# Start of an attention and MLP kernel: the zeros of the first products are cleared first, and the first q is loaded over three queues, ahead of the identity

## The chip, the cores and the metric

One core of one Trainium2 chip runs the whole program. The metric is device time in microseconds, the median of several runs. Engines are called as in the profile: PE (TensorE, with PEld for its weight loads), DVE (VectorE), ACT (ScalarE), POOL (GpSimd) and SP (SyncE, which here only issues DMAs). POOL, SP and ACT each issue DMAs in the order of their own program.

## The reference

```
scores = q @ k.T / sqrt(64)              # 4 x 12 heads, 448 x 448, head size 64
scores = cap * tanh(scores / cap)        # cap = 30
attn   = exp(scores - max) / (sum + 1e-9)
x      = (attn @ v), heads side by side  # 1792 x 768
h      = relu(x @ w_in)                  # w_in  768 x 2048, float64
out    = (h * h) @ w_out                 # w_out 2048 x 768, float64
```

## The kernel before, in words

The twelve heads of each of four batches are taken in pairs: 24 steps `n`, each with two heads. A head has 448 keys and 448 queries, which lie on the partitions as seven blocks of 64. Products that must be exact are made of float32 values split in a high and a low part (`hi`, `lo`, tiles `kqh` and `kql`), in three products.

In one step of the main loop PE transposes the next pair's k and q (`transpose_k`, `transpose_q`, lines 334 to 345), against the identity matrix `ident`, into PSUM. `take` (lines 347 to 354) splits the result; `scores` (L362) multiplies k by q; ACT applies tanh (L369) and exp (L374); `pv` and `pv_half` (L397, L389) multiply by v. Weights of the MLP are decoded from float64 beside that, and the MLP's first products (`hps`, L286) begin while attention still runs. The second products of the MLP (`po`, L654 to L656) end the program.

Ahead of the main loop stands a prologue, and the change lies wholly in it:

- `make_identity` (its lines carry the name masks.py in the profile) fills `ident` on POOL: a memset of zeros (masks.py:197), then an affine select that writes the ones of the diagonal (masks.py:199).
- DVE clears padding of the k and v buffers and writes ones beside v (L231 to L237), and then `zero` (L433).
- PE multiplies `zero` by `zero` NWARM = 9 times into a PSUM tile `warm` that nobody reads (L436); the profile shows each of these products as two matmuls.
- `load_k(0)`, `load_q(0)` (L305, L306, L315, L316) load the first pair, half on SP's queue, half on ACT's. `cap`, the q of step 1, and the v of steps 0 and 1 are loaded on POOL's queue (L440, L315, L316, L305, L306), the k of step 1 and the first weights on SP's.
- The first transposes, the split of their results (`take` with ACT's copy and DVE's subtraction), and some one-column arithmetic on `cap` follow.

The prologue is not written in its order on the engines: a scheduler places each instruction on its engine's list when the program is built, and the engine then runs that list in order. The main loop stands under a manual schedule, in the order in which it is written.

Of the kernel before, what the change touches and what calls it, by code (L numbers as in the profile page):

```python
# [10 lines left out]
F32 = mybir.dt.float32  # L11
# [158 lines left out]
def tile_softcap_attention_mlp(ctx, tc, q, k, v, cap, w_in, w_out, out):  # L170
    nc = tc.nc
# [3 lines left out]
    P = 128  # L175
# [10 lines left out]
    NWARM = 9  # L186
    NKQ = 2
# [18 lines left out]
    g_dram = dram.tile([NF, P, NT], F32, name="g_dram", bufs=1)  # L206

    ident = const.tile([P, P], F32, name="ident")
    make_identity(nc, ident)
    cap_sb = const.tile([P, 1], F32, name="cap_sb")  # L210
    ncap = const.tile([P, 1], F32, name="ncap")
    qks = const.tile([P, 1], F32, name="qks")
# [3 lines left out]
    keep = actx.enter_context(tc.tile_pool(name="keep", bufs=1))  # L216
# [2 lines left out]
    ps_s = actx.enter_context(tc.tile_pool(name="ps_s", bufs=2, space=PSUM))  # L219
    ps_t = actx.enter_context(tc.tile_pool(name="ps_t", bufs=1, space=PSUM))  # L220
    ps_v = actx.enter_context(tc.tile_pool(name="ps_v", bufs=2, space=PSUM))

# [2 lines left out]
    kn, qn, vn = [], [], []  # L227
# [71 lines left out]
    top, bottom = slice(0, D), slice(D, P)  # L299
# [8 lines left out]
    def load_k(n, queues=(nc.sync, nc.sync)):  # L308
        load_keys(kn[n % NKQ], k, n, queues)

    def load_q(n, queues=(nc.sync, nc.sync)):
        b, j = divmod(n, NPAIR)
        for i in range(2):
            x = q[b, 2 * j + i].rearrange("(p t) d -> p t d", t=NS)
            queues[i].dma_start(out=qn[n % NKQ][top, 0:4, i], in_=x[:, 0:4])  # L315
            queues[i].dma_start(out=qn[n % NKQ][bottom, 0:3, i], in_=x[:, 4:7])  # L316

    def load_v(n):
        load_keys(vn[n % NKV][:, :, :, 0], v, n, (nc.gpsimd, nc.gpsimd))
# [108 lines left out]
        last["dve"] = nc.vector.tensor_sub(out=lo, in0=x, in1=hi.bitcast(F32))  # L428
        xh[b, j], xl[b, j] = hi, lo


    zero = keep.tile([P, P], F32, name="zero")
    nc.vector.memset(zero, 0.0)  # L433
    warm = ps_t.tile([P, 512], F32, tag="t", name="warm")
    for _ in range(NWARM):
        nc.tensor.matmul(out=warm[:, :P], lhsT=zero, rhs=zero, start=True, stop=True)  # L436
    both, pool = (nc.sync, nc.scalar), (nc.gpsimd, nc.gpsimd)
    load_k(0, both)
    load_q(0, both)
    nc.gpsimd.dma_start(out=cap_sb, in_=cap.partition_broadcast(P))  # L440
    load_k(1)
    load_q(1, pool)
    load_v(0)
    load_v(1)
# [37 lines left out]
    with tc.manual_schedule(engines={E.PE, E.Activation, E.DVE, E.Pool}):  # L482
# [13 lines left out]
        for n in range(NP + 1):  # L496
# [54 lines left out]
            if n + 2 < NP:  # L551
                load_k(n + 2)
                load_q(n + 2)
                load_v(n + 2)
# [165 lines left out]
```

## Time and profile before

| | |
|---|---|
| runs, us | 719.66, 720.54, 721.70 (median 720.54) |
| profiled execution, us | 720.83 |
| its span, first to last instruction, us | 719.1 |
| mean granted clock of TensorE | 0.994 |
| busy: PE, DVE, ACT, POOL | 98%, 58%, 44%, 12% |

The profiled execution took 720.83 us, of which 719.1 us lie between its first and its last instruction; the other 1.7 us lie around them. Busy shares are of the span. All stretches below are in microseconds from the start of the span. A "granted clock" of 1.00 stands for 2.4 GHz and 0.50 for 1.2 GHz.

### The profile page before, as it was taken

What the parts mean: (1) busy time and instruction counts of PE and PEld (TensorE: products, weight loads), DVE (VectorE), ACT (ScalarE), POOL (GpSimd) and SP (SyncE); (2) the same over time, 40 slices, a digit from 0 to 9 for tenths busy, and PEclk for the clock granted to TensorE, in tenths of its full rate; (3) what the DMA queues carried; (4) which work ended last, traced back from release to release, by engine and by line L of the source; (5) the groups of instructions that cost most, each with busy time, mean ns of one, the idle gap of its engine ahead of it and who ended that gap; (6) DMA issues with size and microseconds to landing.
All of it is one profiled execution on the core that took longest, in us unless ns stands there. A gap on an engine that the chain in (4) does not pass through costs nothing.

```text
span 719.1 us, 10204 instructions
## 1 busy us (share of the span) xinstructions
PE 701.3 (98%) x3642; PEld 589.7 (82%) x3642; DVE 414.3 (58%) x882; ACT 315.8 (44%) x454; POOL 88.6 (12%) x131
## 2 busy tenths in 40 slices
PE   6999999999999999999999999999999999999995
PEld 4655666666566679989999999999999999999995
DVE  4687878778776664548899989419971111111100
ACT  5787777678766743135344444224432111111100
POOL 6432334234232002010000000000000000000000
PEclk9999999999999999999999999999999999999998
DMA  8335544354343033137456454436645232222111
GB/s 168 94 92 123 120 111 114 90 129 111 96 117 100 16 82 136 65 131 223 152 171 192 156 194 157 150 110 183 186 122 152 81 87 80 81 81 82 27 29 27
DMA packets 110334, 83.01 MB, mean 115 GB/s; under 512 B 56449, under 2 KB 100993, under 8 KB 110273
## 3 DMA queue, kind: packets, MB, share of 16 engines
q1 hardware_dynamic: 103840, 73.53, 36.2%
q0 software_dynamic: 3232, 5.74, 3.4%
q10 hardware_dynamic: 3200, 2.98, 1.3%
q8 instruction: 31, 0.51, 0.3%
q14 instruction: 31, 0.25, 0.1%
HBM read 61.87 MB, written 20.27 MB: 114 GB/s over the span
## 4 chain that ended last, share of the span: by engine, by line
PE 91%; DVE 4%; ACT 1%; DMA 1%; issue 1%; SPq 0%; ACTq 0%
PE hps L286 33%; PE pv L397 14%; PE po L654 11%; PE po L655 11%; PE po L656 11%; PE sc L362 7%; PE pv L389 2%; PE tp L338 1%; DVE kql L354 1%; DVE kqh L353 1%; PE sc L344 1%; ACT p L369 1%; DMA kn<-in_k_dram 1%; PE warm L436 1%; PE sc L345 0%
## 5 line engine op out<-in xcount | busy, mean ns | idle before, releaser
L286 PE MATMUL hps<-xs,kqh 128*128 128x448 f32 x576 | 163.7, 365 | 1.3 <-DVE r L291 1.3
L654 PE MATMUL po<-ohi,gh 128*128 128x384 f32 x448 | 149.7, 335 | 0.6 <-ACT osb L661 0.6
L655 PE MATMUL po<-olo,gh 128*128 128x384 f32 x448 | 150.0, 335 | 0.0
L656 PE MATMUL po<-ohi,gl 128*128 128x384 f32 x448 | 148.4, 335 | 0.0
L397 PE MATMUL pv<-p,vn 128*128 128x448 f32 x288 | 122.1, 560 | 0.0
L286 PEld LDWEIGHTS hps<-xs,kqh 128*128 128x128 f32 x576 | 108.1, 188 | 10.2 <-DVE r L291 1.7
L369 ACT ACTIVATE p<-sc,qks 128x896 f32<-128x896 f32 (+1 forms) x96 | 86.7, 904 | 57.5 <-DVE kql L354 42.0
L286 PE MATMUL hps<-xs,kql 128*128 128x448 f32 x288 | 105.2, 365 | 0.0
L607 DVE TENSOR_TENSOR gl<-graw,gh 128x2048 fp32r<-128x2048 f32 x14 | 32.1, 2292 | 124.1 <-ACT gh L606 114.3
L397 PEld LDWEIGHTS pv<-p,vn 128*128 128x128 f32 x288 | 51.2, 191 | 51.3 <-issue 42.1
L374 ACT ACTIVATE p<-p,cap_sb 128x896 f32<-128x896 f32 (+1 forms) x96 | 91.3, 951 | 2.1
L654 PEld LDWEIGHTS po<-ohi,gh 128*128 128x128 f32 x448 | 84.0, 188 | 0.9 <-ACT osb L661 0.9
L655 PEld LDWEIGHTS po<-olo,gh 128*128 128x128 f32 x448 | 84.1, 188 | 0.0
L656 PEld LDWEIGHTS po<-ohi,gl 128*128 128x128 f32 x448 | 83.9, 188 | 0.0
L290 ACT ACTIVATE r<-hps 128x448 f32<-128x448 f32 x64 | 34.6, 541 | 76.2 <-PE hps L286 74.5
L606 ACT CAST gh<-graw 128x2048 fp32r<-128x2048 f32 x14 | 26.7, 1910 | 91.9 <-PE po L655 81.8
L291 DVE TENSOR_TENSOR r<-hps,r 128x448 f32<-128x448 f32 x64 | 39.7, 621 | 43.2 <-ACT r L290 43.1
L44 ACT ACTIVATE mag<-wraw 128x384 f32<-128x384 f32 x64 | 34.8, 552 | 53.4 <-DVE olo L56 31.0
L286 PEld LDWEIGHTS hps<-xs,kql 128*128 128x128 f32 x288 | 54.1, 188 | 4.3
L286 PE MATMUL hps<-xs,whi 128*128 128x448 f32 x192 | 56.1, 372 | 0.0
L362 PE MATMUL sc<-kqh 64*128 64x448 f32 (+1 forms) x168 | 43.6, 441 | 2.9 <-ACT p L369 2.0
L661 ACT COPY osb<-po 128x384 f32<-128x384 f32 x28 | 13.2, 477 | 69.9 <-PE po L656 59.2
(85 smaller groups left out, 843.2 us busy)
## 6 DMA issues: line engine op xcount, KB each, us to landing
g_dram<-r SPq DMA_DIRECT2D x64, 224.0 KB, 2.5
graw<-g_dram SPq DMA_DIRECT2D x14, 1024.0 KB, 5.8
wraw<-in_moe_w_in_dram SPq DMA_DIRECT2D x32, 384.0 KB, 4.0
wraw<-in_moe_w_out_dram SPq DMA_DIRECT2D x32, 384.0 KB, 3.6
rb<-rd SPq DMA_DIRECT2D x24, 224.0 KB, 3.5
vn<-in_v_dram POOLq DMA_DIRECT2D x48, 64.0 KB, 3.4
kn<-in_k_dram SPq DMA_DIRECT2D x47, 64.0 KB, 2.6
qn<-in_q_dram SPq DMA_DIRECT2D x45, 64.0 KB, 2.6
```

Of the source, the lines that this page charges most:

```text
L44: yield nc.scalar.activation(out=magf, in_=high.bitcast(F32), func=ACTF.Abs, scale=2.0 ** 16)
L286: nc.tensor.matmul(out=ps, lhsT=w[:, c * P:(c + 1) * P], rhs=x[b, c], start=(n == 0), stop=(n == 3 * KDM - 1))
L290: nc.scalar.activation(out=r, in_=ps, func=ACTF.Relu)
L291: last["square"] = nc.vector.tensor_mul(out=r, in0=ps, in1=r)
L362: nc.tensor.matmul(out=sc[:, h, :S], lhsT=kx[r, t * P:(t + 1) * P], rhs=qx[r, 4 * P:], start=(s == 0), stop=(s == 2))
L369: nc.scalar.activation(out=p, in_=probs[n, u][:, :c, :S], func=ACTF.Tanh, scale=qks)
L374: nc.scalar.activation(out=p, in_=p, func=ACTF.Exp, scale=cap_sb)
L397: nc.tensor.matmul(out=pvs[n, h], lhsT=vs[:, u - 1, h].rearrange("p a d -> p (a d)"), rhs=p[:, h], start=(u == 1), stop=(u == 3))
L607: nc.vector.tensor_sub(out=gl, in0=graw, in1=gh.bitcast(F32))
L654: nc.tensor.matmul(out=po[:, o, :HO], lhsT=gh, rhs=hi[:, os_], start=(f == 0), stop=False)
L655: nc.tensor.matmul(out=po[:, o, :HO], lhsT=gh, rhs=lo[:, os_], start=False, stop=False)
L656: nc.tensor.matmul(out=po[:, o, :HO], lhsT=gl, rhs=hi[:, os_], start=False, stop=(f == NF - 1))
```

## The change

Two pieces of the prologue move, and the queues of one load change.

```diff
     ident = const.tile([P, P], F32, name="ident")
-    make_identity(nc, ident)
...
     ps_v = actx.enter_context(tc.tile_pool(name="ps_v", bufs=2, space=PSUM))
+
+    zero = keep.tile([P, P], F32, name="zero")
+    nc.vector.memset(zero, 0.0)
+    warm = ps_t.tile([P, 512], F32, tag="t", name="warm")
+    for _ in range(NWARM):
+        nc.tensor.matmul(out=warm[:, :P], lhsT=zero, rhs=zero, start=True, stop=True)
...
-    def load_q(n, queues=(nc.sync, nc.sync)):
+    def load_q(n, upper=(nc.sync, nc.sync), lower=None):
         b, j = divmod(n, NPAIR)
         for i in range(2):
             x = q[b, 2 * j + i].rearrange("(p t) d -> p t d", t=NS)
-            queues[i].dma_start(out=qn[n % NKQ][top, 0:4, i], in_=x[:, 0:4])
-            queues[i].dma_start(out=qn[n % NKQ][bottom, 0:3, i], in_=x[:, 4:7])
+            upper[i].dma_start(out=qn[n % NKQ][top, 0:4, i], in_=x[:, 0:4])
+            (lower or upper)[i].dma_start(out=qn[n % NKQ][bottom, 0:3, i], in_=x[:, 4:7])
...
-    zero = keep.tile([P, P], F32, name="zero")
-    nc.vector.memset(zero, 0.0)
-    warm = ps_t.tile([P, 512], F32, tag="t", name="warm")
-    for _ in range(NWARM):
-        nc.tensor.matmul(out=warm[:, :P], lhsT=zero, rhs=zero, start=True, stop=True)
     both, pool = (nc.sync, nc.scalar), (nc.gpsimd, nc.gpsimd)
     load_k(0, both)
-    load_q(0, both)
+    load_q(0, (nc.gpsimd, nc.scalar), (nc.gpsimd, nc.sync))
+    make_identity(nc, ident)
     nc.gpsimd.dma_start(out=cap_sb, in_=cap.partition_broadcast(P))
```

What the scheduler makes of it is seen in the engines' lists. Line numbers of the changed kernel are higher by 5 or 6 in the load functions (L305 becomes L311, L315 becomes L321). First POOL's list before, from its first row after the branch to the program: `qn1` is the q of step 1, `vn0` the v of step 0.

```order
masks.py:197 MEMSET ident_79 128x128
L440 DMA cap_sb_84<-in_cap_dram 128x1
L315 DMA qn1_112<-in_q_dram 64x4x64
L316 DMA qn1_112<-in_q_dram 64x3x64
masks.py:199 ISA
masks.py:199 AFFINE_SELECT ident_79<-ident_79 128x128
L315 DMA qn1_112<-in_q_dram 64x4x64
L316 DMA qn1_112<-in_q_dram 64x3x64
L305 DMA vn0_115<-in_v_dram 64x4x64
```

The affine select stands behind three DMA issues. In the changed kernel POOL's list begins so (`qn0` is the q of step 0):

```order
L321 DMA qn0_116<-in_q_dram 64x4x64
L322 DMA qn0_116<-in_q_dram 64x3x64
masks.py:197 MEMSET ident_79 128x128
L441 DMA cap_sb_80<-in_cap_dram 128x1
L321 DMA qn1_120<-in_q_dram 64x4x64
L322 DMA qn1_120<-in_q_dram 64x3x64
```

Two more issues of `qn1` follow, four of `vn0` and two of `vn1`, and then these rows (`vn1` and `vn2` are the v of steps 1 and 2):

```order
L311 DMA vn1_127<-in_v_dram 64x3x64
L312 DMA vn1_127<-in_v_dram 64x4x64
masks.py:199 ISA
masks.py:199 AFFINE_SELECT ident_79<-ident_79 128x128
L311 DMA vn2_131<-in_v_dram 64x4x64
```

The affine select has moved behind fifteen DMA issues: the two of the first q, the one of `cap`, four of the next q, and eight of v. PE's list, with what each row waits for, begins in the changed kernel with the products of zeros and the transposes of k, then those of q (`Pool`, `DVE` and `PE` are the engines' semaphores, DMAHW those of loads from SP and ACT, DMASW those of loads from POOL):

```order
L227 MATMUL warm<-zero 128x128 [waits DVE_49]
L227 MATMUL warm<-zero 128x128 x8
L344 MATMUL tp<-ident,kn_115 128x128 [waits DMAHW1_49,DMAHW2_49,DMAHW0_49,DMAHW3_49,PE_49,Pool_49]
L344 MATMUL tp<-ident,kn_115 128x128 x2
L344 MATMUL tp<-ident,kn_115 128x128 [waits DVE_49]
L350 MATMUL tp<-ident,qn_116 128x128 [waits DMAHW4_49,DMAHW5_49,DMASW1_49,DMASW0_49]
```

Before, the transposes of q stood ahead of those of k; the first transposes wait for POOL, that is for `ident`, in both kernels. On DVE the clearing of `zero` moves from behind twelve memsets to the head of the list. On ACT and on SP one load of the first q goes to POOL from each pair of theirs; SP's reading of the flag `far` (L597, L598 in the changed kernel) moves from behind the loads of steps 2 and 3 to ahead of them. From the first scores on, the lists of PE, DVE, ACT and POOL are the same in both kernels.

## Rows read from the trace of the kernel before

**Rows 1.** The profile's page: busy time, share of the span and instructions of each engine; and the shares of the span in the chain of work that ended last, by engine.
```profile
PE 701.3 (98%) x3642; PEld 589.7 (82%) x3642; DVE 414.3 (58%) x882; ACT 315.8 (44%) x454; POOL 88.6 (12%) x131
...
PE 91%; DVE 4%; ACT 1%; DMA 1%; issue 1%; SPq 0%; ACTq 0%
```

**Rows 2.** The chain that ended last, in order of time, in the first 20 us: start, duration, what. Consecutive pieces follow one another without a gap.
```profile
0.83 0.11 DVE kn L231
...
4.05 0.15 DVE zero L433
4.20 0.04 issue
4.25 4.02 PE warm L436 x18
8.27 0.33 PE tp L344 x3
...
8.83 0.54 ACT kqh L353
...
9.40 0.62 DVE kql L354
...
10.04 0.70 DVE kql L354
...
10.79 0.49 PE sc L362 x2
...
11.30 1.02 ACT p L369
...
12.34 1.05 ACT p L374
13.39 0.90 ACT p L369
...
15.21 3.20 PE pv L397 x8
```

**Rows 3.** The timeline of POOL in the first 12 us: start, duration, engine, line, operation. Between 3.58 and 11.52 stand twelve more DMA issues with no gap.
```profile
0.75 0.20 POOL masks.py:197 MEMSET ident<- 128x128 f32 x1 [0.29 <-POOLq L702]
1.30 0.72 POOL L440 DMA_DIRECT2D cap_sb<-in_cap_dram  x1 [0.34 <-issue]
2.02 0.63 POOL L315 DMA_DIRECT2D qn<-in_q_dram  x1
2.63 0.62 POOL L316 DMA_DIRECT2D qn<-in_q_dram  x1
3.34 0.30 POOL masks.py:199 TENSOR_SCALAR_AFFINE_SELECT ident<-ident 128x128 f32<-128x128 f32 x1
3.58 0.64 POOL L315 DMA_DIRECT2D qn<-in_q_dram  x1
...
11.52 0.63 POOL L306 DMA_DIRECT2D vn<-in_v_dram  x1
```

**Rows 4.** The timeline of PE between 7.9 and 12 us: the transposes of the first q and k.
```profile
8.10 0.49 PE L344 MATMUL tp<-ident,qn 128*128 128x128 f32 x3
...
8.73 0.66 PE L338 MATMUL tp<-ident,kn 128*128 128x128 f32 x4
```

**Rows 5.** The timeline of the first 20 us, all engines: the third DMA issue of ACT and of SP.
```profile
2.20 0.64 ACTq L315 DMA_DIRECT2D qn<-in_q_dram  x1
...
2.47 0.64 SPq L315 DMA_DIRECT2D qn<-in_q_dram  x1
```

**Rows 6.** Busy time of each engine by stretch: the stretch, its length, then PE, PEld, DVE, ACT, POOL busy (with the number of instructions), the granted clock of TensorE, the busy share of the DMA engines, GB/s.
```profile
4.25:8.30 4.05, 4.05 (x20) 4.05 (x21) 0.87 (x8) 0.78 (x2) 4.05 (x7) 1.00 1.11 199
...
66.00:69.00 3.00, 1.57 (x13) 0.97 (x12) 1.50 (x5) 2.74 (x4) 0.00 (x0) 1.00 0.39 87
69.70:72.60 2.90, 2.90 (x9) 1.54 (x8) 2.80 (x6) 2.87 (x4) 1.00 (x1) 0.50 0.12 23
...
711.40:714.50 3.10, 0.00 (x0) 0.00 (x0) 0.00 (x0) 0.48 (x1) 0.00 (x0) 1.00 0.28 74
714.50:719.10 4.60, 0.00 (x0) 0.00 (x0) 0.00 (x0) 0.00 (x0) 0.00 (x0) 0.50 0.03 7
```

**Rows 7.** The chain that ended last, in order of time, between 60 and 76 us: products with v in the stretch of the lower granted clock.
```profile
70.72 2.75 PE pv L397 x4
```

**Rows 8.** DMA issues of the first 12 us by tile and queue: number, KB each, median us from issue to landing.
```profile
qn<-in_q_dram POOLq DMA_DIRECT2D x2, 64.0 KB, 3.9
...
qn<-in_q_dram SPq DMA_DIRECT2D x1, 48.0 KB, 4.3
cap_sb<-in_cap_dram POOLq DMA_DIRECT2D x1, 0.5 KB, 3.3
```

**Rows 9.** Who waited for whom, PE alone, from 8 us to the end: us in total, times, longest.
```profile
PE sc L362 <- ACT p L369: 2.0, 3, 0.7
PE hps L286 <- DVE r L291: 1.3, 1, 1.3
PE pv L389 <- DVE vl L324: 1.1, 2, 0.6
```

**Rows 10.** Groups of instructions by line and form in the first 15 us, ACT's copy of the first k: busy time, mean ns of one, idle time before it.
```profile
L353 ACT CAST kqh<-tp 128x512 fp32r<-128x512 f32 x1 | 0.6, 585 | 0.1
```

**Rows 11.** Who waited for whom, SP's queue, first 30 us: us in total, times, longest.
```profile
SPq L305 <- PE tp L338: 1.6, 1, 1.6
```

## The prediction

> **What bounds the kernel now.** I read the page's busy shares first, then the chain that ended last. PE is busy for 701.3 of 719.1 us, and 91% of the chain lies on it [rows 1]: a reader should see that whatever makes PE start its real work later is paid at the end in full, unless a wait further on gives it back. PE's waits behind the start are few, and each is released by ACT or DVE (2.0, 1.3 and 1.1 us) [rows 9], whose work comes from PE's own products, so they move along with it. None waits for a clock of its own, such as a long load. I take it that a delay at the start reaches the end one to one.
>
> Then the chain of the first microseconds, which is where the change lies. DVE clears `zero` last of its memsets, ready at 4.20; the products of zeros run from 4.25 to 8.27; the transposes of q follow at once [rows 2]. So before, the first transposes wait for the products of zeros, and these for DVE. `ident` is no part of that chain: its affine select starts at 3.34 and lasts 0.30, so it is there by 3.65 [rows 3], 4.4 us before the first transpose at 8.10 [rows 4].
>
> **The change, part by part.**
>
> *Zeros first.* The products of zeros can start some 3.2 us earlier: DVE's first memset begins at 0.83 [rows 2], `zero` takes 0.15 to 0.17, so PE starts near 1.05 and, at the 4.02 us of before [rows 2], ends near 5.1. Taken alone this is the gain of the change, at most 3.2 us. The other memsets move back by 0.17 us, hidden behind loads that land later.
>
> *The first q.* It loses one issue each on ACT and SP and gets two on POOL. Landing takes 3.9 us from POOL and 4.3 from SP [rows 8]. With the first issue on POOL at 0.75 and the third ones on ACT and SP at about 2.2 and 2.5 [rows 5], all of k and q is there by about 6.8 us. With the zeros done at 5.1, the transposes would start at 6.8 instead of 8.1 if loads were all they waited for.
>
> *The identity.* They aren't. POOL's list puts the affine select behind fifteen DMA issues, and in the trace POOL is held by each issue: in a row of them the next starts 0.61 us later (3.58 to 11.52 is thirteen steps, 7.94 us), and the affine select of before started only when the three issues ahead of it were over, at 3.34 after 2.63 plus 0.62 [rows 3]. So I add up: start 0.75; two issues of the first q at 0.72 (the first on this queue) and 0.62, to 2.09; the memset 0.20 and the pause of 0.34 that followed it, to 2.63; `cap` 0.62, to 3.25; twelve issues at 0.61, to 10.58; a gap of 0.09 ahead of the affine select and its 0.30, to 10.97; a few hundredths to PE. The first transpose starts at about 11.0 instead of 8.1: **+2.9 us**. Bounds: without the pause and with 0.60 per issue 10.5 (+2.4); with 0.64 per issue and some 0.3 of waits for an earlier load's semaphore 11.7 (+3.6). I take the middle, since the row of thirteen steps is the very same kind of issue on the same queue.
>
> *The order of k and q.* k's transposes now come first. From the first transpose to the last wait of the first scores, before: 8.08 to 10.79, 2.71 us [rows 2]. After: k's transposes 0.66 [rows 4], ACT's copy of k 0.585 [rows 10] and of q 0.54, then DVE's second subtraction, 0.62 for q [rows 2], with some 0.1 of steps between: about 2.6. DVE's subtraction of k, 0.70 [rows 2], runs beside ACT's copy of q. I cost it at nothing.
>
> *TensorE's clock.* PE now stands idle from about 5.1 to 11.0. The trace shows what such idleness does: the last product ends at 711.4, the granted clock stays at 1.00 to 714.5, and from there it is 0.50, the 1.2 GHz level [rows 6]. It even fell inside the loop, at 69.7, behind a stretch of 3 us in which PE was busy for 1.57 [rows 6]. So I take the low level for the first work behind the pause. What that costs: four products with v took 2.75 us in the low stretch [rows 7], eight took 3.20 in the other [rows 2], 0.69 against 0.40 each. On the path at the start stand k's transposes (0.66, doubled less a little overlap: +0.55) and the last pair of the first scores (0.49: +0.45), so +1.0. Behind that ACT needs 1.02, 1.05 and 0.90 us for tanh, exp and tanh [rows 2], 2.97 in all, and PE has some 2.7 us of products in this time; doubled they stick out by up to 2.4 us if the level doesn't rise. In the trace it was low for 2.9 us in the loop [rows 6], and at the start it rose within the 4.02 us of the zeros. The path behind the first transpose reaches the end of the first scores about 4 us later, so I let most of ACT's cover hold and take **+1.2 us**, between 0 (the level is up again at once) and 3.4 (1.0 and 2.4).
>
> The granted clock of the very start reads 1.00 [rows 6], and yet the 18 matmuls of zeros took 4.02 us [rows 2], 0.223 us for 128 columns, where eight products with v took 0.40 for 448, that is 0.114 for 128: half the speed, so the low level, which the column doesn't show there. The Trainium skill ("TensorE: Matmul & The Clock Gate", Part 1) says that the slow clock is the default and that "activity releases the throttle". By the granted clock of that row the pause would cost nothing and the sum would be 723.4; by the page's rule it costs a second ramp, 724.6; the durations of these rows bear out the rule.
>
> *The rest.* SP reads `far` earlier, a single instruction ahead of the k loads of step 2, which wait for the first transposes of k anyway (1.6 us) [rows 11]: nothing. The v loads of step 2 leave POOL about 2 us later, and are wanted two steps on: nothing. `cap` is issued at 2.63 instead of 1.30, lands 3.3 us later [rows 8], and is wanted by the first tanh, near 15: nothing.
>
> **The sum.** 720.83 (the profiled execution, of which 719.1 is the span) plus 2.9 plus 1.2 is 724.9. That execution stands 0.29 above the median of the three runs, 720.54; on the median's footing I predict **724.6 us**. About 0.3%, 2.2 us, is what a measurement of this kernel can tell from no change.
>
> **The rivals.**
>
> - *The clock doesn't matter* (0.10). The identity is late, but the level is high when PE resumes or rises at once. For it speaks the granted clock of 1.00 at the start; against it the fall 3.1 us behind the last product [rows 6]. 720.54 plus 2.9: 723.4.
> - *The low level lasts* (0.06). PE has short pauses for ACT and DVE in its first work, as it had in the 3 us ahead of 69.7 [rows 6], and the level stays low past the cover: 2.9 plus 3.4, 726.8.
> - *A part of the delay is given back* (0.06). One of PE's waits, or the fall at 69.7, which doubles products on the chain [rows 7], doesn't come at the shifted time. The four products alone gave up 1.15 us there, and with their neighbours and a wait of 1.3 it makes up to 2.5: 722.1.
> - *The identity isn't late* (0.04). POOL hands its issues on without being held, and the affine select runs soon after its memset. Then the loads bound the first transpose, at 6.8 instead of 8.1: 720.54 less 1.3 is 719.2, no slower than before. The point from which it decides: the affine select would have to end by 8.0, so fifteen issues would have to cost no more than 0.42 us each (8.0 less 0.30, 0.09, 0.54 and 0.75 is 6.3). The row shows 0.61 and an affine select that waited for the issues ahead of it [rows 3], which is why it gets so little.
>
> The Trainium skill ("DMA: Bandwidth & Descriptors", Issuing engines are not separate DMA queues) has a rule on that side: starting loads on several engines saves only the time of issuing them, which is usually small beside the load. By it the issues would hardly hold POOL, and the last rival would be the likeliest; the 0.61 us of an issue [rows 3] against 3.9 us to landing [rows 8] says that fifteen of them are not small here.
>
> **How the numbers follow.** The forecast has the remaining 0.74. Its own bounds are 2.4 to 3.6 for the identity and, for the larger part, 0.6 to 2.0 for the clock: 723.5 to 726.1. The first three rivals add 722.1 to 726.8, and the fall at 69.7 may come or not in either kernel. The range for 8 times in 10 is **722.4 to 727.0**; the identity in time, and part of the two cases at its ends, are left out. Slower by over 0.3% means above 722.7: nearly all of the forecast, most of the first rival and the second, 0.87. Within 0.3%: the identity in time, most of the part given back, and a few hundredths of the others, 0.11. Faster by over 0.3%, below 718.4: only if an identity in time meets a clock that never falls, 0.02.
>
> **What would show it right or wrong.** In the changed kernel's POOL timeline the affine select should start at about 10.7, right behind the eighth load of v, and the first transpose at about 11.0; PE's zeros should run from about 1.05 to 5.1, and then nothing for nearly 6 us. The chain should begin with POOL's issues instead of DVE's memsets. The granted clock should read 0.50 for a few us at the start, and k's first four transposes take about 1.2 instead of 0.66. From there the timeline should be that of before, shifted by about 4 us to the end. I am wrong on the identity if the affine select starts before 9, on the clock if the first transposes run at 0.66, and on carrying the delay if the last product doesn't end 3 to 5 us later than 711.4.

## The result, and the profile after

The changed kernel takes 725.40 us, the median of six runs from 724.68 to 726.30; beside it the kernel before took 721.34 (719.66 to 721.85). The medians differ by 4.1 us. The ratio on record is 1.0061, with a 95% interval of 1.0048 to 1.0074: slower. Like all ratios below it is worked out from the single runs, and can differ from the quotient of the two medians by up to 0.2%. The profiled execution took 725.12 us with a span of 723.4, against 720.83 and 719.1.

The page's first row and its chain by engine, which answer to [rows 1], show PE still busy nearly throughout, with 1.2 us more of work and a span that is 4.3 us longer:

```profile
PE 702.5 (97%) x3642; PEld 590.9 (82%) x3642; DVE 414.5 (57%) x882; ACT 315.6 (44%) x454; POOL 90.2 (12%) x133
...
PE 89%; DVE 5%; DMA 2%; ACT 1%; issue 1%; SPq 1%; ACTq 0%
```

Then the timeline of POOL in the changed kernel, which answers to [rows 3]: start, duration, line, operation, and in brackets the idle time before it and what ended it.

```profile
1.28 0.76 POOL L321 DMA_DIRECT2D qn<-in_q_dram  x1 [0.82 <-POOLq L703]
2.03 0.63 POOL L322 DMA_DIRECT2D qn<-in_q_dram  x1
2.65 0.22 POOL masks.py:197 MEMSET ident<- 128x128 f32 x1
2.79 0.59 POOL L441 DMA_DIRECT2D cap_sb<-in_cap_dram  x1
3.38 0.62 POOL L321 DMA_DIRECT2D qn<-in_q_dram  x1
...
10.09 0.62 POOL L312 DMA_DIRECT2D vn<-in_v_dram  x1
10.81 0.30 POOL masks.py:199 TENSOR_SCALAR_AFFINE_SELECT ident<-ident 128x128 f32<-128x128 f32 x1
```

Twelve issues lie from 3.38 to the end of the one at 10.09, 0.61 us each, and only then comes the affine select. It ends at 11.11. PE in the same stretch, which answers to [rows 4]:

```profile
1.07 4.21 PE L227 MATMUL warm<-zero 128*128 128x128 f32 x18 [1.07 <-DVE zero L224]
11.16 1.12 PE L344 MATMUL tp<-ident,kn 128*128 128x128 f32 x4 [5.88 <-DMA wraw<-in_moe_w_in_dram]
12.07 0.85 PE L350 MATMUL tp<-ident,qn 128*128 128x128 f32 x3
...
13.84 0.74 PE L368 MATMUL sc<-kqh 64*128 64x448 f32 x2 [0.62 <-ACT kqh L359]
...
15.04 0.58 PE L368 MATMUL sc<-kqh,kql 64*128 64x448 f32 x2
```

and the first weight loads of the transposes:

```profile
11.16 0.72 PEld L344 LDWEIGHTS tp<-ident,kn 128*128 128x128 f32 x4 [6.18 <-POOL ident masks.py:199]
```

The zeros run from 1.07 to 5.28, PE stands idle for 5.88 us, and four transposes take 1.12 us instead of 0.66. The two rows name different releasers: the row of the matmuls a load of weights that happened to land at 11.14, the row of the weight loads POOL's `ident`, ready at 11.11. The chain of the changed kernel follows the first of the two and shows 4.69 us of that load, and not POOL's issues, as I had forecast. A chain follows whatever came last, to a few hundredths of a microsecond, and can be led away by a coincidence; the experiments with the identity settle which of the two it was.

The first tanh of ACT answers to the piece at 11.30 in [rows 2]:

```profile
15.66 1.01 ACT L375 ACTIVATE p<-sc,qks 128x896 f32<-128x896 f32 x1 [1.87 <-PE sc L368]
```

It comes 4.36 us later. From there I laid ACT's first tanh of each step side by side in the two timelines:

| step | before, us | after, us | later by |
|---|---|---|---|
| 0 | 11.30 | 15.66 | 4.36 |
| 3 | 38.49 | 42.85 | 4.36 |
| 5 | 58.76 | 62.87 | 4.11 |
| 6 | 69.81 | 74.56 | 4.75 |
| 9 | 99.69 | 103.97 | 4.28 |
| 12 | 131.94 | 136.28 | 4.34 |
| 23 | 249.44 | 253.79 | 4.35 |

The last product starts at 715.38 instead of 711.03, 4.35 us later; the first line is of the changed kernel, the second of the kernel before:

```profile
715.38 0.34 PE L657 MATMUL po<-ohi,gl 128*128 128x384 f32 x1
```

```profile
711.03 0.34 PE L656 MATMUL po<-ohi,gl 128*128 128x384 f32 x1
```

So in this pair of executions the loss is complete before the first tanh and stays to the end. Only steps 5 to 9 wander, between 4.11 and 4.75 us, as is described below under the rival that a part is given back.

### The profile page after: what moved, and what is told of

The parts are those of the page before. It is cut to its first block, busy times and chain, and to the rows that moved or that the text cites. A ratio compares the mean times of both kernels' runs of the same rounds, so it can differ in the third digit from the quotient of the medians.

```text
span 723.4 us, 10209 instructions
## 1 busy us (share of the span) xinstructions
PE 702.5 (97%) x3642; PEld 590.9 (82%) x3642; DVE 414.5 (57%) x882; ACT 315.6 (44%) x454; POOL 90.2 (12%) x133
## 4 chain that ended last, share of the span: by engine, by line
PE 89%; DVE 5%; DMA 2%; ACT 1%; issue 1%; SPq 1%; ACTq 0%
PE hps L292 33%; PE pv L403 13%; PE po L655 11%; PE po L656 11%; PE po L657 11%; PE sc L368 7%; PE pv L395 2%; PE tp L344 1%; DVE kql L360 1%; DMA cmp<-e 1%; DVE kqh L359 1%; PE sc L350 1%; DVE x L430 1%; DMA wraw<-in_moe_w_in_dram 1%; ACT p L375 1%
```

## The experiments

All times are medians; "before" was run beside each group, with 721.05, 721.07 and 721.25 us in the three groups. The first table collects what the sections speak of: the start of the affine select, of the first transposes and of the first tanh in the profile, and the ratio to before with its 95% interval. A profiled execution is one of the runs and need not lie at the median: e1's is the slowest of its seven, 720.27, and so is b3's, 720.60.

| kernel | affine select | first transpose | first tanh | median | ratio to before |
|---|---|---|---|---|---|
| before | 3.34 | 8.10 | 11.30 | 721.34 | |
| changed | 10.81 | 11.16 | 15.66 | 725.40 | 1.0061 (1.0048 to 1.0074) |
| e1, identity early | 3.37 | 5.34 | 9.48 | 718.91 | 0.9968 (0.9955 to 0.9981) |
| e2, zeros only | 3.35 | 5.41 | 11.47 | 720.83 | 0.9993 (0.9982 to 1.0003) |
| e7, queues only | 3.36 | 8.24 | 11.44 | 720.29 | 0.9996 (0.9988 to 1.0005) |
| e6, behind seven | 5.94 | 6.30 | 10.79 | 719.89 | 0.9989 (0.9978 to 1.0000) |
| e5, behind eleven | 8.39 | 8.76 | 13.24 | 723.29 | 1.0030 (1.0021 to 1.0038) |
| e4, 36 zeros | 10.81 | 12.11 | 15.38 | 723.91 | 1.0039 (1.0024 to 1.0055) |
| e8, 31 zeros | 10.80 | 11.16 | 14.46 | 723.38 | 1.0028 (1.0016 to 1.0040) |
| b1, v ahead | 3.38 | 5.43 | 9.07 | 723.33 | 1.0034 (1.0017 to 1.0050) |
| b2, v ahead, 13 zeros | 3.39 | 6.43 | 9.94 | 721.68 | 1.0008 (0.9994 to 1.0021) |
| b3, q of step 1 split | 3.36 | 5.52 | 9.80 | 719.39 | 0.9968 (0.9957 to 0.9979) |
| b4, the same, 11 zeros | 3.37 | 5.43 | 9.35 | 718.92 | 0.9985 (0.9966 to 1.0004) |

**The identity early.** The changed kernel, with nothing but the identity's place on POOL's list undone:

```diff
-    make_identity(nc, ident)
+    with tc.high_priority():
+        make_identity(nc, ident)
```

> The changed kernel with the identity alone given priority: POOL's list has its memset first and its affine select behind three DMA issues instead of fifteen; zeros first and the three queues stay. My theory (POOL is held 0.61 us by each issue ahead of the affine select, and TensorE's clock falls in the long pause): the affine select starts near 3.4, the loads bound the first transpose at about 6.8, the pause behind the zeros is only 1.5 us and the transposes run at 0.66 for four. 1.3 us below the kernel before, about 720.0 by a median of 721.3. Rival one, that it is q's way over POOL's queue that is late: the first transpose stays near 11 and the time near 725.4. Rival two, that the clock falls even in a short pause: about 721.3, like before.

PE's timeline:

```profile
1.07 4.12 PE L227 MATMUL warm<-zero 128*128 128x128 f32 x18 [1.07 <-DVE zero L224]
5.34 0.63 PE L344 MATMUL tp<-ident,kn 128*128 128x128 f32 x4
6.33 0.52 PE L350 MATMUL tp<-ident,qn 128*128 128x128 f32 x3 [0.37 <-DMA qn<-in_q_dram]
...
8.33 0.73 PE L368 MATMUL sc<-kql,kqh 64*128 64x448 f32 x2 [0.18 <-DVE kql L360]
```

The time falls to 718.91, 6.5 us below the changed kernel and 2.1 below before, where I had expected 1.3. So the identity's place on POOL's list is what turned the change from a gain to a loss, and it was `ident`, not the load of weights, that released the transposes. The loads of q bound them now, at 6.33 rather than the 6.8 I expected. The first rival is refuted. Of the second a part is true: the clock was up for the first transposes (0.63 for four) and low again in the first scores (0.73, then 0.58 for a pair), but the time isn't the 721.3 that it named. Where the 2.1 us come from no trace shows: in the profiled execution, the slowest of the seven, the first tanh comes 1.82 us sooner than before, that of step 1 only 0.63, and the last product 0.33 (710.70). A part of the lead is lost to v:

```profile
PE pv L403 <- DMA vn<-in_v_dram: 0.7, 2, 0.4
```

**Single parts.** The zeros first alone (the clearing and the products of zeros move together), and then the three queues alone, each on the kernel before:

```diff
     ps_v = actx.enter_context(tc.tile_pool(name="ps_v", bufs=2, space=PSUM))
+    zero = keep.tile([P, P], F32, name="zero")
+    nc.vector.memset(zero, 0.0)
...
-    zero = keep.tile([P, P], F32, name="zero")
-    nc.vector.memset(zero, 0.0)
...
     both, pool = (nc.sync, nc.scalar), (nc.gpsimd, nc.gpsimd)
```

> The kernel before with only the clearing of zero and its products moved first; q on SP and ACT, the identity early. My theory: zeros end near 5.2, the last load of q (fourth issue on SP at 3.15, 4.3 us to landing) bounds the first transpose at about 7.5 instead of 8.1, so 0.6 us below before, about 720.7. Against the run with the identity early it prices the three queues alone, 0.7 us. Rival (zeros first is what costs, since the clock falls before the transposes): 1 us or more above before.

The chain of that run:

```profile
3.14 4.48 DMA qn<-in_q_dram
7.62 0.24 issue
7.86 0.87 PE tp L349 x3
```

As expected the fourth issue on SP bounds the transposes of q, at 7.86. But they ran at the low level, 0.87 for three, and so had those of k, which follow the zeros directly:

```profile
5.41 1.09 PE L343 MATMUL tp<-ident,kn 128*128 128x128 f32 x4
```

The first tanh came at 11.47, 0.17 later than before. The median is 0.2 us lower, not to be told from none: for the zeros alone no gain is shown.

```diff
-    load_q(0, both)
+    load_q(0, (nc.gpsimd, nc.scalar), (nc.gpsimd, nc.sync))
```

> The kernel before with only the first q over three queues; identity early, zeros last. Theory: the first transposes still wait for the zeros, at 8.1, so nothing is gained; POOL issues two loads more ahead of v, so the v of step 0 comes 1.2 us later, and since the first product with v waited 0.3 us for it before, up to 1.2 us are lost: 721.1 to 722.3. Rival (the three queues are a gain of their own): below 720.4.

The median, 720.29, lies below the 720.4 that the rival had named, but before stood at 721.07 beside it and the interval of the ratio reaches 1, so no gain is shown. Nor does the start show one: the zeros end at 8.41, against 8.27 before, and the first tanh comes 0.14 us later. Nothing was lost either: PE's list of waits in that run holds none for v. The 1.2 us that I allowed for the later v were not paid: it was issued 1.2 us later and still in time.

**How many issues ahead.** The changed kernel with v's loads put behind the affine select, those of steps 1 and 2 (eleven issues stay ahead, the diff) or also `load_v(0)` under the same `issue_after` (seven):

```diff
-    make_identity(nc, ident)
+    nc.gpsimd.memset(ident, 0.0)
+    ones = nc.gpsimd.affine_select(out=ident, in_=ident, compare_op=ALU.not_equal, fill=1.0, base=0,
+                                   pattern=[[-1, P]], channel_multiplier=1)
...
-    load_v(1)
+    with tc.issue_after(ones.ins):
+        load_v(1)
...
-                load_v(n + 2)
+                with tc.issue_after(ones.ins):
+                    load_v(n + 2)
```

> The changed kernel with the v loads of steps 1 and 2 put behind the affine select on POOL's list: it stands behind eleven issues instead of fifteen. My theory: it starts 4 x 0.61 us earlier, at 8.4, and the first transpose at 8.7. The pause behind the zeros is then about 3.4 us, near what ended with a fall at the end of the program (3.1), so the clock is open: with a fall 723.0, without 721.7. Rival, that the affine select waits for loads to land and not for issues: it starts at another time than 8.2 to 8.6. Rival, that only a handful of issues ahead matter: it stays near 10.8 and the time near 725.4.

> The changed kernel with all v loads put behind the affine select: it stands behind seven issues. By the 0.61 us an issue (10.81 behind fifteen, 8.39 behind eleven) it should start at 5.95 and end at 6.26, just when the last load of the first q is there (6.3 with the identity early). So this is the point from which the identity stops to bound: first transposes at 6.3, about 0.4 us later than with the identity early (719.3 against 718.9). If the identity were still the bound in another way (a fixed lateness behind any load), it would lie well above 720.

The affine select in the two runs, eleven issues first:

```profile
8.39 0.31 POOL L441 TENSOR_SCALAR_AFFINE_SELECT ident<-ident 128x128 f32<-128x128 f32 x1
```

```profile
5.94 0.31 POOL L441 TENSOR_SCALAR_AFFINE_SELECT ident<-ident 128x128 f32<-128x128 f32 x1
```

and the first transposes behind them, in the same order:

```profile
8.76 1.11 PE L344 MATMUL tp<-ident,kn 128*128 128x128 f32 x4 [3.47 <-POOL ident L441]
```

```profile
6.30 1.12 PE L344 MATMUL tp<-ident,kn 128*128 128x128 f32 x4 [1.02 <-POOL ident L441]
```

With 10.81 behind fifteen that is 2.42 and 2.45 us for four issues, 0.61 each: POOL is held by the issue, not by the landing. Both forecasts of the start hold to 0.02 us. Behind eleven the first transpose comes at 8.76, the level is low (1.11 for four transposes) and the median 723.29, near the 723.0 of the case with the low level. Behind seven, `ident` is ready when the last load of q is, but it still bounds the start: the transposes of k, which began at 5.34 with the identity early, wait for it until 6.30 and then run at the low level, and the first tanh comes 1.31 us later than there. The median is 719.89, against the 719.3 expected and 718.91 with the identity early. So seven issues are not yet the point from which the identity costs nothing.

**The clock.** The changed kernel with more products of zeros, so that PE has no pause, or a short one, ahead of the identity; first 36, then 31:

```diff
-    NWARM = 9
+    NWARM = 36
```

> The changed kernel with 36 products of zeros instead of 9, nothing else. My theory: 9 to 10 of them at the low level to about 5, the others at 0.21 us each, to about 10.7; the first transpose stays at 11.16, since the identity bounds it, but the clock is up: four transposes of k in 0.66 instead of 1.12, first tanh 3.2 us behind the first transpose instead of 4.5. 1.3 us below the changed kernel, about 724.1. Rival, that the 1.3 us come from the order of k and q or from loads beside them and not from the clock: 725.4, tanh still 4.5 behind. If the zeros run past 11.1 the gain is smaller by what they run over.

> The changed kernel with 31 products of zeros: with 36 they ran on to 12.0, past the identity (11.1), since the low level lasted longer than I had reckoned. At 0.213 us each five fewer end at 10.9. Then the identity bounds the first transpose again, at 11.16, and only the clock differs from the changed kernel: first tanh 3.25 us behind the first transpose, at 14.4, instead of 15.66; 1.25 us below the changed kernel, about 724.1, or 3.0 above before. Rival (the clock is not what makes the difference of 1.3): 725.4.

With 36 they ran to 12.0, past the identity, because the low level lasted longer than I had reckoned; the first transpose came 0.95 us late. From there to the first tanh it is 3.27 us, against 4.50 in the changed kernel, but the price of the clock is not read cleanly from it. With 31:

```profile
1.07 9.26 PE L227 MATMUL warm<-zero 128*128 128x128 f32 x62 [1.07 <-DVE zero L224]
11.16 0.66 PE L344 MATMUL tp<-ident,kn 128*128 128x128 f32 x4 [0.83 <-POOL ident masks.py:199]
11.65 0.49 PE L350 MATMUL tp<-ident,qn 128*128 128x128 f32 x3
...
12.96 0.47 PE L368 MATMUL sc<-kqh 64*128 64x448 f32 x2 [0.62 <-ACT kqh L359]
...
14.05 0.36 PE L368 MATMUL sc<-kqh,kql 64*128 64x448 f32 x2
```

```profile
14.46 1.01 ACT L375 ACTIVATE p<-sc,qks 128x896 f32<-128x896 f32 x1 [1.55 <-PE sc L368]
```

The first transpose starts at 11.16, as in the changed kernel to the hundredth, and the first tanh at 14.46 instead of 15.66. So 1.20 us of the loss are TensorE's clock, and the order of k and q and the loads beside it are not to blame. The medians differ by 2.0 us, 0.8 more, and whether that too is the clock is not shown. In the two profiles e8 is ahead of the changed kernel by 1.20 us at the first tanh of step 0 and by 1.22 in step 3, behind it by 0.62 in steps 4 and 5, and ahead by 1.64 from step 6 on: 0.4 us of the rest come in where both wander.

**A better version.** With the identity early PE waited 0.7 us for v, as shown above. Two ways to bring v forward: ahead of the q of step 1, or with a part of that q on ACT's queue.

```diff
     load_k(1)
-    load_q(1, pool)
     load_v(0)
+    load_q(1, pool)
     load_v(1)
```

> Identity early, zeros first, three queues, and on POOL's list the v of step 0 ahead of the q of step 1. With the identity early the first tanh came 1.82 us sooner than before, the second only 0.63: PE waited 0.7 us for v at the first products with v. With v four issues (2.4 us) sooner this wait should go: 718.2 against 718.9. Rival: the q of step 1, now 2.4 us later, is waited for instead, and nothing is gained or something lost.

> As the run with v ahead, with 13 products of zeros instead of 9, so that PE has no pause between the zeros and the last load of q (5.2 to 6.3). If the low level in the first scores (products of 0.58 instead of 0.37 us) comes from these pauses, it goes in most executions, and the first tanh comes up to 0.7 us sooner: about 717.5. If the level's return hangs on something else than these pauses: 718.2 to 718.9, as without.

The rival came true, that q is then waited for. PE's timeline in the run with nine zeros:

```profile
13.66 0.52 PE L350 MATMUL sc<-ident,qn 128*128 128x128 f32 x3 [2.66 <-DMA qn<-in_q_dram]
```

The first tanh was the earliest of all, at 9.07, and was given back to a wait of 2.66 us for the q of step 1, whose loads were issued from 6.1 to 8.5 and took 4.6 to 5.7 us to land. The first tanh of step 1 came only 0.17 us sooner than before. With 13 zeros this wait is 2.46. Both medians lie above before, that of b2 by an amount not told from none. The wait explains why the lead is gone, not why b1's median is 2.3 us above before: the profiled execution, 720.70, is the second fastest of twelve that reach from 720.17 to 725.92. The six with a mean granted clock of 0.991 or 0.992 took 722.51 to 725.92, so a longer time at the low level goes with much of the loss; no trace shows where. The other way:

```diff
-    load_q(1, pool)
+    load_q(1, (nc.gpsimd, nc.scalar))
```

> The run with the identity early, and one head of the q of step 1 on ACT's queue instead of POOL's: v's issues move 1.2 us forward without putting q of step 1 back. With the identity early PE waited 0.7 us for v at the first products with v; if that is what gave back the early start, about 0.6 us below that run, 718.3. Rival, that the loads are bound by what the DMA engines move and not by their issue: the same as that run, 718.9.

> As the run with q of step 1 split, with 11 products of zeros instead of 9, so that they reach to the last load of the first q (6.3). If the pause between 5.2 and 6.3 is what lets the clock fall in the first scores of some executions, a few tenths below that run, about 718.0; if not, the same within 0.3.

The wait for v is gone, and the first tanh of step 1 comes 1.49 us sooner than before instead of 0.63. Yet the median is 719.39, a ratio of 0.9968, just that of the identity early alone. In its profile, the slowest execution of the seven, the lead is 1.52 us in step 3, 0.90 in step 4 and gone in step 6; PE waits for ACT and DVE there:

```profile
PE sc L368 <- ACT p L375: 2.2, 3, 0.7
PE pv L403 <- DVE e L409: 0.7, 1, 0.7
```

(who waited for whom, between 40 and 76 us: us in total, times, longest; before, the first of these is 1.4 us and the second isn't there). With 11 zeros the first scores ran at the high level (0.36 for a pair) and the median is 718.92, 0.5 us lower, between the two outcomes that I had named; but two of its twelve executions took 724.7 and 724.8, and why I can't say; its interval reaches 1. The version to take is the change with the identity given priority: 718.91 us, 0.32% below before and 0.9% below the changed kernel; the split of q adds nothing that these runs can tell.

## Why the prediction was right, point by point

- *What bounds the kernel, and the delay carried to the end.* Right in this pair: 4.36 us at the first tanh, 4.35 at the last product. That they agree so closely is partly luck. In most other profiles the distance to the one profile of before changed between steps 3 and 12: e4 to e8 gained 0.3 to 0.6 us there, e1 and b4 lost 0.3, and b3 lost the whole of its lead of 1.52. Forecast were 4.1 on the profiled execution's footing; measured 4.3 there and 4.06 on the medians, with before itself at 721.34 in the larger set of runs.
- *Zeros first.* Forecast 1.05 to 5.1, measured 1.07 to 5.28. The gain of 3.2 us, which I had called the most that it could give, was not had: alone it gave 0.2, not told from none.
- *The first q.* Forecast at 6.8, with the identity early 6.33.
- *The identity, +2.9.* Measured +3.06 (8.10 to 11.16); the affine select at 10.81 against about 10.7. One term was misplaced: I put a pause of 0.34 behind the memset, as in [rows 3]. In the changed kernel the memset is followed by an issue at once, and the first issue starts at 1.28 instead of 0.75. POOL's first DMA issue began at 1.28 to 1.31 in every profile here, whether or not the memset stood ahead of it, so the pause goes with the first issue. The two slips were of 0.53 and 0.34 us and nearly cancelled.
- *The order of k and q, nothing.* With the clock up, 3.30 us from the first transpose to the first tanh (e8) against 3.20 before: 0.1. (The 8.08 of that sum stands in no row; the first transpose starts at 8.10.)
- *The clock, +1.2.* Measured 1.20 (e8 against the changed kernel), but of other parts than I had added up, so that the exact number is luck. I had 1.0 on the path to the first tanh (0.55 for k's transposes, 0.45 for the last pair of scores) and the rest behind it. Measured are 0.42 for k's transposes (q's start at 12.07 against 11.65, with the same start of k's), 0.46 for q's, which I had left out (13.84 against 12.96 adds up to 0.88), 0.2 for the last pair, 0.1 between, and nothing behind the first tanh. What the runs don't tell is whether the level fell in the pause or had not yet risen when the ninth product of zeros was over: these take 4.21 us for 18 matmuls in the changed kernel, the low rate throughout; in e2, with the same 4.21 us, the transposes right behind them ran low; and in e6 the level is low behind a pause of just 1.0 us. I had spoken of a fall.
- *The rule on the clock.* "TensorE: Matmul & The Clock Gate" (the Trainium skill, Part 1) says that the slow clock is the default. The durations agree: with the low level behind the pause the sum came to 724.6, 4.1 us above before, without it to 723.4, 2.9 above, and 4.06 were measured on the medians. One of my signs failed: the granted clock, which should have read 0.50 for a few us at the start, reads 1.00 in the changed kernel too, while a pair of score products takes 0.58 us instead of 0.36 (the columns as in [rows 6]):

```profile
15.00:16.00 1.00, 1.00 (x8) 0.88 (x7) 0.00 (x0) 0.34 (x1) 0.00 (x0) 1.00 0.80 196
```

  The Trainium skill ("DMA: Bandwidth & Descriptors", Issuing engines are not separate DMA queues) says that the time of issuing is usually small beside the load. This list is a case where it isn't: fifteen issues of about 0.61 us held POOL for 9 us.
- *The rivals.* The clock that doesn't matter: refuted by e8. The identity in time: refuted; e1 shows what it would have given, 718.91 against the 719.2 I had worked out. The low level that lasts: PE's products ran low from 11.16 to about 17.3, and ACT's third tanh slipped a further 0.47 us (20.38 against 15.55), but at the first tanh of step 1 the delay was back at 4.35, since before ACT had waited 0.41 us for PE there; the 2.4 us that could have stuck out of ACT's cover were not paid. The part given back rested on the fall at 69.7 [rows 6], which I priced at 1.15 us and more. The changed kernel has no such fall, as this stretch shows (length, busy time of PE, PEld, DVE, ACT and POOL, granted clock, DMA share, GB/s, as in [rows 6]):

```profile
68.00:72.00 4.00, 2.93 (x11) 1.41 (x12) 2.78 (x5) 1.02 (x2) 0.00 (x0) 1.00 0.42 101
72.00:76.00 4.00, 3.27 (x21) 1.77 (x18) 3.57 (x10) 3.93 (x6) 1.20 (x1) 1.00 0.34 73
```

  and yet it is as late in step 12 as in step 0. Before, four products with v took 2.75 us there in the chain [rows 7], now 1.77 in the timeline:

```profile
74.96 1.77 PE L403 MATMUL pv<-p,vn 128*128 128x448 f32 x4
```

  In this pair of executions the difference bought nothing. From 72 to 76 us DVE is busy for 3.57 of 4 us and PE for 3.27, so PE is probably not the bound there; that is argued from busy shares and was not tested. Such a stretch may still cost something as a rule: of the 79 executions of before beside the experiments, the 13 with a mean granted clock of 0.995 or less have a median of 721.70, the other 66 one of 721.00. A doubled row on the chain need not be a loss of its full length.

## What to carry to other kernels

Where an engine both computes and issues DMAs, count the issues ahead of each computation on its list: here each cost POOL 0.61 us, and a scheduler that moved one 0.3 us instruction behind twelve more of them turned a gain of 2.1 us into a loss of 4.1 us; in the profiles 3.1 us of the loss are the later first transpose and 1.2 the clock behind it. Look at the list that was built, not at the order of the source, and give priority to what the first real work waits for. And before a start is brought forward, follow the next load behind it: with v ahead of q the wait only moved, from 0.7 us for v to 2.7 us for q.

## What the runs showed that I had not expected

- The time that products of zeros run at the low level differs: reckoned, as an estimate, from 0.213 us a matmul at the low rate and 0.107 at the high, of 9.26 us about 5.0 were low with 31 products, of 10.93 us about 6.2 with 36, and all of the 4.2 us in the changed kernel; with 11 (b4) the first transposes behind them ran at the high level.
- The same load can land much later when it is issued later on POOL: with v ahead, the q of step 1 took 4.6 to 5.7 us from issue to landing, where it had taken 3.9 in the kernel before [rows 8]. Whether it is the loads ahead of it or those of other queues that hold it up was not tested.
